# A Fourier layer and a token and channel mixer on one core: the 47-point products of the stream's last two units in three rounded passes, with the weight tasks on fewer steps and some early work in another order

## The chip, the core and the metric

The kernel runs on one core of a Trainium2 chip. Its engines work side by side, each through its own queue in order: TensorE (PE, with its weight loads as PEld), VectorE (DVE), ScalarE (ACT), GpSimd (POOL) and SyncE (SP), which issues most of the transfers (DMA). The metric is the device time of one execution in microseconds (us); the number that is compared is the median of several runs.

## The reference

For 8 batches of 3008 tokens with 256 channels, all in fp32:

```python
X = np.fft.rfft(x, axis=1)
Yr = Xr @ w_r - Xi @ w_i + b_r
Yi = Xr @ w_i + Xi @ w_r + b_i
Y  = soft_threshold(Yr, 0.01) + 1j * soft_threshold(Yi, 0.01)
x  = np.fft.irfft(Y, n=3008, axis=1)
h  = np.maximum(x.transpose(0, 2, 1) @ w_tok1, 0.0) @ w_tok2   # over tokens, 256 wide
u  = x + h.transpose(0, 2, 1)
out = u + np.maximum(u @ w_ch1, 0.0) @ w_ch2                   # over channels, 1536 wide
```

## The kernel before

The transform of length 3008 is done as 47 times 64. A *47-point product* multiplies a row of 120 sums or differences of inputs (13 rows a unit) by a constant matrix `f1`; its results go to DRAM (`a_d`) and come back, per pair of frequencies `kp` (12 pairs), for the 64-point step, the mix with `w_r` and `w_i`, the synthesis with the matrices `e` (the `inverse`, L501 and the passes in L208 to L210 with `pi` as output) and the first token product (`tokens`, output `gp`).

The batches are five units: 0 is one batch, done first in plain fp32 by `begin`; units 1, 2 and 3 are two batches each (512 columns) and unit 4 is one (256 columns), done by `stream`. In the stream most products are *rounded*: an operand is split into a high part (a cast on ACT) and a low part (a subtraction), and three matmuls high*high, high*low, low*high (`mm3`, L208 to L210) take the place of one fp32 matmul. The 47-point products are still plain fp32 (L278). The stream has 84 steps, one for each unit, `kp` and batch (24 each for units 1 to 3, 12 for unit 4). While a unit is in its steps, the 13 rows of the *next* unit's 47-point products are put between them by `row47`: it loads the input of row n+3 (`load`), forms sums and differences of row n+2 (`add`: the sums on POOL, L265; the differences on DVE, L266, or on POOL for units 3 and 4), and multiplies row n (`product`). Unit 1's own rows run late in `begin`.

Beside the steps the stream does *tasks*: it widens and splits the weights of the later stage (`w_ch1`, `w_ch2`, `w_tok2`, which come as pairs of 32-bit words: tile `wide`, DVE L175 to L182 and L720 to L731, split into `so`). Every task has a cost, and `pace`, the sum of costs over `TASK1 - TASK0` steps, says how much of them is due in a step from `TASK0` on. In unit 1's steps it also splits the synthesis matrices (`split_e`, tile `et`, ACT and DVE) and stores them (`es_d`) for the later units, and splits the token weights of unit 0 (`split_w`, ACT and POOL).

`begin` first does unit 0's 47-point products (L293), then, beside unit 0's steps, widens `w_tok1` and transforms it (L280, L281, stored as `a_w`), and from its step n = `NW` = 10 on reads `a_w` back (`load_w`, tile `aw`) and does its 64-point step (`transform`, L356). After the stream comes the *channel stage* (L905, L939 and the lines after them).

The written order isn't the order on the engines: a layer of the language sorts the instructions of each engine by readiness, except those pinned with `keep_in_program_order`; a tile pool with `bufs=n` makes the writer of a buffer wait for the readers of the buffer n before it. A queue never overtakes: what stands behind a waiting instruction waits with it.

## Time and profile before

| | |
|---|---|
| median of 3 runs | 2298.2 us (2296.5 to 2304.86) |
| the profiled execution: its time, its span | 2290.62 us, 2288.8 us |
| PE busy | 2252.3 us (98%), 11740 matmul records |
| DVE busy | 1951.2 us (85%) |
| ACT busy | 1630.9 us (71%) |
| POOL busy | 293.8 us (13%), all of it before 690 us |
| DMA | 407.87 MB, 178 GB/s in the mean |

All times of the trace count from the span's start; the profiled execution took 1.8 us more than its span. The span falls into `begin` (to 172 us), the stream (172 to about 680 us) and the channel stage (to the end). The stream's units begin, by their first L538 product, at 172.4, 311.8, 460.1 and 595.5 us.

### The profile page before, as it was taken

The numbers are of one execution on the slowest core, as the hardware profiler recorded it, in microseconds if no ns is written. First come the engines' busy times: TensorE is split into PE (matmuls) and PEld (weight loads), VectorE is DVE, ScalarE is ACT, GpSimd is POOL, SyncE is SP. The second block draws the span as 40 slices with busy tenths as digits, with TensorE's granted clock in tenths as the row PEclk, the third lists the DMA queues.
The fourth block names the chain that finished last, engine by engine and source line by source line (L and its number), as shares of the span: only waits on it lengthen the run. The fifth ranks groups of instructions, "written<-read, shape, count | busy, mean of one in ns | idle before, by whom it ended". The sixth has DMA issues, their size and how long they took to land.

```text
span 2288.8 us, 33922 instructions
## 1 busy us (share of the span) xinstructions
PE 2252.3 (98%) x11740; PEld 1911.8 (84%) x11740; DVE 1951.2 (85%) x3228; ACT 1630.9 (71%) x3103; POOL 293.8 (13%) x262
## 2 busy tenths in 40 slices
PE   8899999999999999999999999999999999999998
PEld 7767888899997888888888888888888888888887
DVE  7626877778747999989999998999998999998999
ACT  5446776666647777777777777777777777777776
POOL 0125755454330000000000000000000000000000
PEclk9999999999999999999999999999999999999999
DMA  7789978776677543454444445444454444444435
GB/s 215 226 281 304 303 240 274 240 243 219 192 225 243 162 153 121 147 171 152 139 144 146 124 148 177 147 141 149 120 160 142 153 146 142 139 147 143 143 109 159
DMA packets 205609, 407.87 MB, mean 178 GB/s; under 512 B 17093, under 2 KB 108829, under 8 KB 205437
## 3 DMA queue, kind: packets, MB, share of 16 engines
q1 hardware_dynamic: 175369, 351.69, 50.0%
q10 hardware_dynamic: 30068, 54.01, 7.0%
q8 instruction: 93, 1.52, 0.3%
q14 instruction: 79, 0.65, 0.1%
HBM read 303.00 MB, written 102.63 MB: 177 GB/s over the span
## 4 chain that ended last, share of the span: by engine, by line
PE 86%; DMA 5%; DVE 5%; ACT 2%; issue 1%; POOL 1%; SPq 1%; ACTq 0%; POOLq 0%; DVEq 0%
PE s L939 28%; PE sx L939 16%; PE sw L939 8%; PE pu L939 5%; PE pu L905 5%; PE fq L939 4%; PE p L554 4%; PE p L278 3%; PE px L538 2%; PE pm L554 2%; DMA x<-in_x 1%; PE gp L208 1%; PE gp L209 1%; PE gp L210 1%; DMA raw<-in_wt 1%
## 5 line engine op out<-in xcount | busy, mean ns | idle before, releaser
L939 PE MATMUL s<-rh,a2s 128*128 128x512 f32 (+1 forms) x2016 | 773.1, 386 | 1.5 <-ACT rh L154 0.8
L939 PE MATMUL sx<-ub,a 128*128 128x512 f32 (+1 forms) x1728 | 485.4, 389 | 1.8 <-DVE c L995 1.1
L939 PEld LDWEIGHTS s<-rh,a2s 128*128 128x128 f32 x2016 | 377.6, 188 | 78.8 <-ACT rh L154 1.6
L157 DVE TENSOR_TENSOR rl<-c,rh 128x512 fp32r<-128x512 f32 (+1 forms) x576 | 380.5, 674 | 38.6 <-ACT rh L154 30.8
L939 PE MATMUL s<-rl,a2s 128*128 128x512 f32 (+1 forms) x1008 | 389.2, 386 | 0.8 <-DVE rl L157 0.2
L154 ACT CAST rh<-c 128x512 fp32r<-128x512 f32 (+1 forms) x576 | 340.8, 613 | 57.0 <-DVE c L1036 18.3
L939 PEld LDWEIGHTS sx<-ub,a 128*128 128x128 f32 x1728 | 315.7, 188 | 62.6 <-DVE c L995 1.9
L939 PE MATMUL sw<-ub,a 128*128 128x512 f32 (+1 forms) x864 | 239.1, 385 | 0.4 <-ACT c L976 0.4
L939 PEld LDWEIGHTS s<-rl,a2s 128*128 128x128 f32 x1008 | 189.4, 188 | 40.0 <-DVE rl L157 2.9
L1064 DVE TENSOR_TENSOR uf<-s,uf 128x512 f32<-128x512 f32 (+1 forms) x288 | 194.0, 674 | 18.1 <-PE s L939 17.6
L154 ACT CAST rh<-r 128x512 fp32r<-128x512 f32 (+1 forms) x288 | 174.2, 612 | 37.5 <-PE s L939 25.6
L157 DVE TENSOR_TENSOR rl<-r,rh 128x512 fp32r<-128x512 f32 (+1 forms) x288 | 189.0, 672 | 4.1 <-ACT rh L154 3.1
L939 PEld LDWEIGHTS sw<-ub,a 128*128 128x128 f32 x864 | 160.8, 188 | 34.5 <-ACT c L976 0.8
L911 ACT COPY uf<-pu 128x470 f32<-128x470 f32 (+31 forms) x158 | 61.0, 415 | 121.3 <-PE pu L905 120.8
L905 PEld LDWEIGHTS pu<-g,b 96*128 96x128 f32 x1024 | 130.7, 191 | 4.1 <-DMA b<-b_d 0.7
L157 POOL TENSOR_TENSOR yl<-z,yh 128x512 fp32r<-128x512 f32 x84 | 114.1, 1359 | 129.7 <-ACT yh L154 128.0
L905 PE MATMUL pu<-g,b 96*128 96x94 f32 x1024 | 129.3, 271 | 0.3 <-DMA b<-b_d 0.3
L1039 DVE SCALAR_TENSOR_TENSOR rl<-c,rh 128x512 fp32r<-128x512 f32 (+1 forms) x144 | 97.4, 677 | 29.1 <-ACT rh L1038 27.9
L939 PE MATMUL fq<-ub,a 128*128 128x512 f32 (+1 forms) x432 | 121.6, 390 | 0.0
L939 PE MATMUL pu<-wt,gh 128*128 128x470 f32 (+1 forms) x424 | 116.7, 356 | 0.0
L976 ACT COPY c<-sw 128x512 f32<-128x512 f32 (+1 forms) x144 | 83.3, 579 | 42.5 <-PE sw L939 40.3
L970 ACT COPY fq<-sx 128x512 f32<-128x512 f32 (+1 forms) x144 | 81.1, 563 | 41.2 <-PE sx L939 39.4
(151 smaller groups left out, 4562.4 us busy)
## 6 DMA issues: line engine op xcount, KB each, us to landing
a2s<-a_d SPq DMA_DIRECT2D x336, 384.0 KB, 3.1
wt<-wt_d SPq DMA_DIRECT2D x32, 940.0 KB, 5.6
out<-uf SPq DMA_DIRECT2D x78, 256.0 KB, 3.1
x<-in_x SPq DMA_DIRECT2D x39, 480.0 KB, 6.2
a<-a_d SPq DMA_DIRECT2D x36, 512.0 KB, 5.8
b_d<-bt ACTq DMA_DIRECT2D x36, 512.0 KB, 4.2
wt<-wt_d SPq DMA_DIRECT2D x24, 752.0 KB, 5.2
a_d<-a ACTq DMA_DIRECT2D x36, 480.0 KB, 5.3
```

The lines of the kernel that those rows point to most:

```text
L154: S.copy(out=hi, in_=src)
L157: lo_eng.tensor_tensor(out=lo, in0=src, in1=hi.bitcast(F32), op=ALU.subtract)
L278: PE.matmul(pt[:120, o:o + w], lhsT=f1[:, i], rhs=sd[:, i], start=True, stop=True)
L538: PE.matmul(pt[:, o:o + 128], lhsT=a2[:, ab, b, t * 128:(t + 1) * 128], rhs=f2cols(2 * kp + ab), start=True, stop=True)
L554: PE.matmul(out, lhsT=xt[x][:, j, t], rhs=w_[:, wsel, t], start=start and t + i == 0, stop=t == 1 and i == 2, skip_group_check=True)
L905: m = PE.matmul(pt[:, s * TOKS:(s + 1) * TOKS], lhsT=b2[:, s, cs], rhs=g2[:, 0 if s0 + s == 0 else 1], start=False, stop=s == k - 1, skip_ ...
L911: S.copy(out=ufs[m][:, ct, lo - at:hi - at], in_=pt[:, lo - c0:hi - c0])
L939: m = PE.matmul(out, lhsT=w, rhs=x, start=start and n == 0, stop=n == 2, skip_group_check=True)
L970: S.copy(out=q, in_=x)
L976: S.copy(out=block(1, k), in_=w)
L1039: V.scalar_tensor_tensor(out=lo, in0=src, scalar=0.0, in1=hi.bitcast(F32), op0=ALU.max, op1=ALU.subtract)
L1064: V.tensor_tensor(out=o, in0=outs[r], in1=o, op=ALU.add)
```

## The change

It has these parts:

- `round`, a new call of `row47` one row ahead of the product, splits the sums and differences of units 3 and 4 (`FIRSTR = 3`) into `hi` (ACT) and `lo` (DVE), 2 x 512 columns a row for unit 3 and 2 x 256 for unit 4, and `stage1` multiplies them with the split constant `f1r` in three passes. `f1r` is split once, in `begin`.
- The tasks run over steps 16 to 78 in place of 3 to 82.
- The synthesis matrices are split in `begin`, after each `inverse` of unit 0, on ACT and POOL in place of ACT and DVE, and stored there; unit 1 reads them back as the later units do. `ef` has three buffers in the pool `early`, `et` three.
- In `begin`, `row47` stands ahead of `tokens` and `transform`, and at n = `NW` its transfers are issued after the loads of `a_w`.
- The first two turned tiles of unit 0 are copied in halves, by DVE and ACT.
- `f1` is loaded through ACT's queue; the pool `deep` lies below `wide` in memory; `ev` moves into `early`.

```diff
-FIRST47 = 7
-TASK0, TASK1 = 3, 82
+FIRST47, FIRSTR = 7, 3
+TASK0, TASK1 = 16, 78
...
+    f1r = mid.tile([120, 2, 2, 128], F32R, name="f1r")
...
-    DMA.dma_start(out=f1w, in_=io["f1"])
+    PUT.dma_start(out=f1w, in_=io["f1"])
...
+                if hi is not None:
+                    mm3(pt[:120, o:o + w], f1r[:, 0, i, :120], f1r[:, 1, i, :120], hi[:, i], sd[:, i], True, True)
+                elif pool is None:
...
-    def split_e(ef, kp):
-        et = wk.tile([128, 2, 2, 128], F32R, name="et")
-        split(et[:, 0], et[:, 1], ef, S, V)
+        et = wk.tile([128, 2, 2, 128], F32R, name="et", bufs=3)
+        split(et[:, 0], et[:, 1], ef, S, G)
...
             if kp < 2:
-                V.tensor_copy(out=a2.rearrange("p k b c -> p (k b c)"), in_=pt)
+                V.tensor_copy(out=flat[:, :C], in_=pt[:, :C])
+                S.copy(out=flat[:, C:], in_=pt[:, C:])
...
+        def round(g):
+            if g < NG and u >= FIRSTR:
+                sd, hi = sums_[g], wc["ys"].tile([120, 2, p.w], F32R, name="hi", bufs=2)
+                lo = wk.tile([120, 2, p.w], F32R, tag="o", name="lo", bufs=4)
+                split(hi, lo, sd, S, V)
+                sums_[g], his[g] = lo, hi
...
-        for k, call in ((n + 3, "load"), (n + 2, "add"), (n, "product")):
+        for k, call in ((n + 3, "load"), (n + 2, "add"), (n + 1, "round"), (n, "product")):
...
                     if u == 1:
                         wts_[kp] = split_w(raw_w.pop(kp), kp)
-                        ets[u, kp] = split_e(raw_e.pop(kp), kp)
                         load_we(kp + 2)
-                    else:
-                        ets[u, kp] = load_split_e(kp)
+                    ets[u, kp] = load_split_e(kp)
...
+                if n == NW + 4:
+                    split(f1r[:, 0], f1r[:, 1], f1w[:, :2], S, V)
...
-                    p.inverse(k, es.pop(k), ys[k], early)
-                    if k + 2 < KP:
-                        es[k + 2] = load_e(k + 2)
+                    while later:
+                        later.pop(0)()
+                    p.inverse(k, es[k], ys[k], early)
+                    split_e(es.pop(k), k)
+                    if k + 3 < KP:
+                        es[k + 3] = load_e(k + 3)
...
                 if n >= FIRST47 and done47["n"] < NG:
-                    row47()
+                    if n == NW:
+                        with tc.issue_after(wc["aw"].ins):
+                            row47()
+                    else:
+                        row47()
+                k = n - NW
+                if k >= 2:
+                    p.tokens(k - 2, wfs1.pop(k - 2), ys[k - 2])
+                if k >= 0:
+                    transform(k)
...
-    with tc.tile_pool(name="wide", bufs=1) as wide, tc.tile_pool(name="deep", bufs=1) as deep, tc.tile_pool(name="ys", bufs=6) as ysp:
+    with tc.tile_pool(name="deep", bufs=1) as deep, tc.tile_pool(name="wide", bufs=1) as wide, tc.tile_pool(name="ys", bufs=6) as ysp:
```

Three places show what this does to the engines' queues. Line numbers of the changed kernel are up to 18 higher for the same code. The first place is on PE in `begin`, at the first product of `transform` (`pw<-aw`). Before, and then with the change:

```order
L483 MATMUL pm<-wf_133,xf 128x256 x2
L483 MATMUL pm<-wsum,xf 128x256 x4
L501 MATMUL pi<-held,ef 128x256 x2
L483 MATMUL pm<-wf_133,xf 128x256 x2
L356 MATMUL pw<-aw,fw 64x256 x4
L278 MATMUL p_950<-sd,f_79 120x512
L278 MATMUL p_953<-sd,f_79 120x512
```

```order
L487 MATMUL pm<-wf_134,xf 128x256 x2
L487 MATMUL pm<-wsum,xf 128x256 x4
L505 MATMUL pi<-held,ef 128x256 x2
L281 MATMUL p_975<-sd,f_79 120x512
L281 MATMUL p_978<-sd,f_79 120x512
L359 MATMUL pw<-aw,fw 64x256 x4
L487 MATMUL pm<-wf_134,xf 128x256
```

Two 47-point products (`p<-sd`) moved from behind the first `pw` to ahead of it, and two products of the mix (`pm<-wf`) from ahead of it to behind it.

The second place is on DVE at the stream's entry, in steps 2 and 3 (`sd<-x` are differences of unit 2's inputs, `xs` and `xtl` belong to the 64-point step, `p` and `z` to the mix). Before, and then with the change:

```order
L545 TENSOR_TENSOR xs<-px,xs 128x256
L547 TENSOR_TENSOR xtl<-px,xth 128x512
L266 TENSOR_TENSOR sd<-x 120x512
L559 TENSOR_TENSOR p_1064<-pm,bias 128x512
L178 TENSOR_SCALAR wide<-raw 128x512
L266 TENSOR_TENSOR sd<-x 120x512
L545 TENSOR_TENSOR xs<-px,xs 128x256
```

```order
L549 TENSOR_TENSOR xs<-px,xs 128x256
L551 TENSOR_TENSOR xtl<-px,xth 128x512
L267 TENSOR_TENSOR sd<-x 120x512
L563 TENSOR_TENSOR p_1106<-pm,bias 128x512
L267 TENSOR_TENSOR sd<-x 120x512
L549 TENSOR_TENSOR xs<-px,xs 128x256
L551 TENSOR_TENSOR xtl<-px,xth 128x512
```

The task's instruction (`wide<-raw`) is gone from here; the two differences still stand ahead of the next step's `xs`.

The third place is on DVE in unit 2, from the `xs` of its fourth step on. Before, and then with the change:

```order
L545 TENSOR_TENSOR xs<-px,xs 128x256
L547 TENSOR_TENSOR xtl<-px,xth 128x512
L567 SCALAR_TENSOR_TENSOR z<-p_1063,z 128x512
L559 TENSOR_TENSOR p_1063<-pm,bias 128x512
L545 TENSOR_TENSOR xs<-px,xs 128x256
L547 TENSOR_TENSOR xtl<-px,xth 128x512
L567 SCALAR_TENSOR_TENSOR z<-p_1064,z 128x512
L559 TENSOR_TENSOR p_1064<-pm,bias 128x512
L178 TENSOR_SCALAR wide<-raw 128x470
L175 TENSOR_SCALAR wide<-wide 128x470
L179 SCALAR_TENSOR_TENSOR wide<-wide 128x470
L545 TENSOR_TENSOR xs<-px,xs 128x256
```

```order
L549 TENSOR_TENSOR xs<-px,xs 128x256
L563 TENSOR_TENSOR p_1106<-pm,bias 128x512
L551 TENSOR_TENSOR xtl<-px,xth 128x512
L157 TENSOR_TENSOR lo<-sd,hi 120x1024
L175 TENSOR_SCALAR wide<-wide 128x512
L571 SCALAR_TENSOR_TENSOR z<-p_1105,z 128x512
L179 SCALAR_TENSOR_TENSOR wide<-wide 128x512
L563 TENSOR_TENSOR p_1105<-pm,bias 128x512
L180 TENSOR_SCALAR wide<-wide 128x512
L157 TENSOR_TENSOR lo<-sd,hi 120x1024
L181 TENSOR_TENSOR wide<-raw,wide 128x512
L178 TENSOR_SCALAR wide<-raw 128x512
```

Twelve rows hold two steps before, and less than one step with the change: two subtractions `lo` of 1024 columns and a task lie between the step's own instructions.

## Rows read from the trace of the kernel before

**Rows 1.** The first line of the page, and the by-engine part of its chain of the work that ended last (shares of the span).

```profile
span 2288.8 us, 33922 instructions
...
PE 86%; DMA 5%; DVE 5%; ACT 2%; issue 1%; POOL 1%; SPq 1%; ACTq 0%; POOLq 0%; DVEq 0%
```

**Rows 2.** Busy time of each engine by stage. Columns: the stretch in us and its length; busy us of PE (instructions), PEld, DVE, ACT, POOL; the granted clock of TensorE as a share of full speed; DMA share; GB/s. The stretches are: all before the stream's first product; the entry to the stream; the rest of unit 1; unit 2; unit 3; and the channel stage.

```profile
0.00:172.40 172.40, 156.43 (x785) 120.69 (x786) 98.70 (x184) 85.72 (x154) 27.62 (x20) 0.97 0.81 241
172.40:205.00 32.60, 28.38 (x160) 22.67 (x158) 16.55 (x30) 18.08 (x39) 17.03 (x14) 0.90 0.97 310
205.00:311.80 106.80, 105.60 (x644) 88.81 (x645) 92.17 (x148) 78.44 (x169) 71.90 (x60) 1.00 0.88 293
311.80:460.10 148.30, 146.05 (x893) 123.21 (x893) 109.95 (x168) 99.77 (x203) 80.69 (x73) 1.00 0.78 249
460.10:595.50 135.40, 134.43 (x895) 123.22 (x894) 104.88 (x179) 92.96 (x193) 65.92 (x68) 1.00 0.69 222
...
690.00:2288.80 1598.80, 1590.75 (x7682) 1346.30 (x7682) 1475.01 (x2423) 1202.99 (x2241) 0.00 (x0) 1.00 0.48 148
```

**Rows 3.** What TensorE waited for between 20 and 172 us: us in total, times, the longest.

```profile
PE pw L356 <- DMA aw<-a_w: 3.8, 1, 3.8
PE px L468 <- ACT bt L504: 2.4, 1, 2.4
PE px L468 <- DVE a L458: 1.8, 1, 1.8
```

**Rows 4.** The timeline of the first 25 us: start us, us, engine, line, operation, names, size, count, and in brackets the idle time ahead of it and who ended it.

```profile
0.74 0.47 SPq L242 DMA_DIRECT2D f<-in_f  x1
...
22.27 1.28 DVE L458 COPY a<-pz 128x512 f32<-128x512 f32 x2
```

**Rows 5.** Groups of instructions by line and shape, over the whole span: count | busy us, mean ns of one | idle time ahead of them: the split of the synthesis matrices on DVE, and a POOL subtraction of the same 256 columns.

```profile
L548 POOL TENSOR_TENSOR xtl<-xs,xth 128x256 fp32r<-128x256 f32 x84 | 65.7, 782 | 78.2 <-ACT xth L546 76.0 <-DMA a<-a_d 1.8
...
L157 DVE TENSOR_TENSOR et<-ef,et 128x256 fp32r<-128x256 f32 x12 | 10.4, 863 | 4.1 <-ACT et L154 4.1
```

**Rows 6.** The same columns as in rows 2, in stretches of 20 us.

```profile
60.00:80.00 20.00, 19.12 (x97) 15.78 (x95) 19.22 (x33) 8.22 (x15) 4.51 (x3) 1.00 0.67 193
...
100.00:120.00 20.00, 16.18 (x73) 11.01 (x72) 7.21 (x10) 6.47 (x13) 4.31 (x3) 0.91 0.78 238
...
180.00:200.00 20.00, 16.84 (x90) 13.26 (x90) 8.08 (x14) 10.14 (x21) 10.71 (x9) 0.85 0.99 312
```

**Rows 7.** The timeline around the first product of the weights' transform (L356).

```profile
103.42 0.33 SPq L440 DMA_DIRECT2D x<-in_x  x1
103.91 3.32 SPq L348 DMA_DIRECT2D aw<-a_w  x3
...
105.66 1.03 PE L483 MATMUL pm<-wf,xf 128*128 128x256 f32 x4
...
110.51 1.09 PE L356 MATMUL pw<-aw,fw 128*64 128x256 f32 x8 [3.82 <-DMA aw<-a_w]
```

**Rows 8.** The timeline of the entry to the stream.

```profile
184.99 0.83 SPq L440 DMA_DIRECT2D x<-in_x  x2
...
185.91 0.43 DVE L178 TENSOR_SCALAR wide<-raw 128x512 uint32<-128x512 uint32 x1 [1.47 <-DMA raw<-in_moe_w_ch]
...
190.01 0.69 DVE L266 TENSOR_TENSOR sd<-x 120x512 f32<-120x512 f32 x1 [3.68 <-DMA x<-in_x]
...
190.15 1.69 POOL L265 TENSOR_TENSOR sd<-x 120x512 f32<-120x512 f32 x1 [5.19 <-DMA x<-in_x]
...
191.78 1.09 PE L278 MATMUL p<-sd,f 120*120 120x512 f32 x2 [1.85 <-DVE xtl L547]
```

**Rows 9.** Pieces of the chain that ended last, in order of time: start us, us, engine, line, count of records. One fp32 product (L278) is two records. At 341 us its operand has 512 columns a product and at 481 us 256; the rounded passes are L208 to L210, with 512 columns at 344 us and 256 at 640 us.

```profile
341.22 1.72 PE p L278 x4
...
344.54 0.24 PE gp L208
344.77 0.23 PE gp L209
345.01 0.23 PE gp L210
...
481.75 0.87 PE p L278 x4
...
640.61 0.12 PE pi L208
```

**Rows 10.** DVE and ACT time of the tasks (all instructions that touch the tile "wide"), in the columns of rows 2 (PE and PEld stand ahead of DVE and are zero; each engine's count is in brackets). The sum is over 172.4 to 690 us.

```profile
311.80:460.10 148.30, 0.00 (x0) 0.00 (x0) 56.20 (x69) 11.58 (x20) 1.00 0.78 249
460.10:595.50 135.40, 0.00 (x0) 0.00 (x0) 51.54 (x81) 11.88 (x24) 1.00 0.69 222
...
sum 517.60, PE 0.00 PEld 0.00 DVE 175.04 ACT 38.24; mean PE 0.00 PEld 0.00 DVE 35.01 ACT 7.65
```

**Rows 11.** DVE subtractions and sums by width: three groups of units 2 and 3 (columns as in rows 5), and the channel stage's subtraction, where POOL has no work (count: shortest/median/longest ns, first and last start).

```profile
L567 DVE SCALAR_TENSOR_TENSOR z<-p,z 128x512 f32<-128x512 f32 x48 | 33.0, 688 | 37.3 <-ACT z L566 37.0
...
L545 DVE TENSOR_TENSOR xs<-px,xs 128x256 f32<-128x256 f32 x48 | 20.1, 419 | 11.4 <-ACT xs L544 11.3
...
L157 DVE TENSOR_TENSOR so<-wide,so 128x470 fp32r<-128x470 f32 x8 | 7.5, 936 | 1.4 <-ACT so L154 1.1
...
L157 DVE TENSOR_TENSOR rl<-c,rh x576: 411/683/695, 702.1 to 2284.7; 128x512 fp32r<-128x512 f32 x185, 128x256 fp32r<-128x256 f32 x7
```

More of the change, by code (lines that the diff above doesn't have):

```diff
@@ L231, in ev @@
     def ev(shape, name):
-        return wk.tile(shape, F32, tag="ev", name=name, bufs=2)
+        return wc["early"].tile(shape, F32, tag="ev", name=name, bufs=2)
     def evs(shape, name):
@@ L263, in sum_diff @@
             return x
-        sd = wk.tile([120, 2, w], F32, tag="o", name="sd", bufs=4) if pool is None else wk.tile([120, 2, w], F32, tag=("xtl", "et")[g % 2], name="sd", bufs=(4, 2)[g % 2])
+        sd = wk.tile([120, 2, w], F32, tag="o", name="sd", bufs=4) if pool is None else wk.tile([120, 2, w], F32, tag=("xtl", "et")[g % 2], name="sd", bufs=(4, 3)[g % 2])
         eng.tensor_tensor(out=sd[:, 0], in0=x[:, 0], in1=x[:, 1], op=ALU.add)
@@ L267, in sum_diff, with stage1 @@
         return sd
-    def stage1(sd, dst, g, w, pool):
+    def stage1(sd, dst, g, w, pool, hi=None):
         n = GS if g < NG - 1 else N2 - GS * (NG - 1)
@@ L276, in stage1 @@
                 o = (i - i0) * w
-                if pool is None:
+                if hi is not None:
+                    mm3(pt[:120, o:o + w], f1r[:, 0, i, :120], f1r[:, 1, i, :120], hi[:, i], sd[:, i], True, True)
+                elif pool is None:
                     PE.matmul(pt[:120, o:o + w], lhsT=f1[:, i], rhs=sd[:, i], start=True, stop=True)
@@ L347, in load_w @@
             aw = wk.tile([128, 2, DT], F32, tag="lw", name="aw")
-        DMA.dma_start(out=aw, in_=src[:, 2 * kp:2 * kp + 2] if src is a_w else src[kp])
+        wc["aw"] = DMA.dma_start(out=aw, in_=src[:, 2 * kp:2 * kp + 2] if src is a_w else src[kp])
         return aw
@@ L363, in load_e @@
     def load_e(kp):
-        ef = wk.tile([128, 2, 128], F32, tag="le", name="ef")
+        ef = wc["early"].tile([128, 2, 128], F32, name="ef", bufs=3)
         DMA.dma_start(out=ef, in_=io["e"][kp].rearrange("p (i j) -> p i j", i=2))
@@ L376, in split_e @@
     def split_e(ef, kp):
-        et = wk.tile([128, 2, 2, 128], F32R, name="et")
-        split(et[:, 0], et[:, 1], ef, S, V)
+        et = wk.tile([128, 2, 2, 128], F32R, name="et", bufs=3)
+        split(et[:, 0], et[:, 1], ef, S, G)
         later.append(lambda: DMA.dma_start(out=es_d[kp], in_=et.rearrange("p a i j -> p (a i j)").bitcast(F32)))
-        return et
     def load_split_e(kp):
-        et = wk.tile([128, 2, 2, 128], F32R, name="et")
+        et = wk.tile([128, 2, 2, 128], F32R, name="et", bufs=3)
         DMA.dma_start(out=et.rearrange("p a i j -> p (a i j)").bitcast(F32), in_=es_d[kp])
@@ L456, in turn @@
             a2 = ld([128, 2, nb, C], "a2")
+            flat = a2.rearrange("p k b c -> p (k b c)")
             if kp < 2:
-                V.tensor_copy(out=a2.rearrange("p k b c -> p (k b c)"), in_=pt)
+                V.tensor_copy(out=flat[:, :C], in_=pt[:, :C])
+                S.copy(out=flat[:, C:], in_=pt[:, C:])
             else:
-                S.copy(out=a2.rearrange("p k b c -> p (k b c)"), in_=pt)
+                S.copy(out=flat, in_=pt)
             return a2
@@ L581, in beside @@
         p = parts_of(u)
-        xs, sums_ = {}, {}
+        xs, sums_, his = {}, {}, {}
         def load(g):
@@ L590, in add @@
                 sums_[g] = sum_diff(xs.pop(g), g, p.w, G, None, G if u > 2 else V)
+        def round(g):
[4 more added lines that the diff above has]
+                sums_[g], his[g] = lo, hi
         def product(g):
             if g < NG:
-                stage1(sums_.pop(g), p.a, g, p.w, None)
-        return SimpleNamespace(load=load, add=add, product=product)
+                stage1(sums_.pop(g), p.a, g, p.w, None, his.pop(g, None))
+        return SimpleNamespace(load=load, add=add, round=round, product=product)
     rows47 = [(u, g) for u in range(1, len(UNITS)) for g in range(NG)]
@@ L621, in stream @@
         a2s, xts, ys, ets = {}, {}, {}, {}
-        wts_, raw_w, raw_e = wc["wts"], {}, {}
+        wts_, raw_w = wc["wts"], {}
         def load_we(kp):
             if kp < KP:
-                raw_w[kp], raw_e[kp] = load_w(w_d, kp), load_e(kp)
+                raw_w[kp] = load_w(w_d, kp)
         def need(i):
@@ L798, in begin @@
             w1 = prepare_w1(early, after)
-            es, xts = {k: load_e(k) for k in range(2)}, {}
+            es, xts = {k: load_e(k) for k in range(3)}, {}
             DMA.dma_start(out=sc, in_=io["scale"])
```

5 lines of the change are left out of this document (removed).

## The prediction, made before the changed kernel was run

> **What bounds the kernel now.** I read the chain that ended last first: 86% of it is TensorE's own work [rows 1]. Then the stages: in the channel stage PE is busy for 1590.75 of 1598.8 us [rows 2], and no instruction of that stage changes, so whatever the change brings lies in the first 690 us. There unit 2 leaves PE idle for 148.3 - 146.05 = 2.3 us and unit 3 for 1.0 us: both are bound by PE's matmuls. The two other places that are left are the waits in `begin` [rows 3] and the entry to the stream, where PE works 28.38 of 32.6 us at a mean granted clock of 0.90 [rows 2]. The reader is to see one more thing in those rows: DVE is busy for 109.95 us of unit 2 and 104.88 us of unit 3, 74% and 77%. It is off the path, but it has only some 35 us to spare in each, and the change spends them.
>
> **The products.** One fp32 product of 512 columns takes 1.72 / 2 = 0.86 us on the chain, one of 256 columns 0.87 / 2 = 0.43 us; three rounded passes take 0.24 + 0.23 + 0.23 = 0.70 us and 3 x 0.12 = 0.36 us [rows 9]. Unit 3 has 13 rows x 2 products of 512 columns, unit 4 the same number of 256: 26 x 0.16 + 26 x 0.07 = 4.2 + 1.8 = **6.0 us less** of PE work, 4.2 of it in unit 2's stretch (the rows go beside the unit ahead of theirs) and 1.8 in unit 3's. That is worth its full size only while PE stays the bound there.
>
> **What DVE pays for it.** First `lo`. A DVE operation takes 419 ns for 256 columns and 688 ns for 512 [rows 11], 269 ns for 256 more; so 1024 columns are some 688 + 2 x 269 = 1.23 us. An operation that reads SBUF alone takes longer while POOL works: `so`, of 470 columns, has a mean of 936 ns, whereas the same subtraction of 512 columns in the channel stage, where POOL has no work, has a median of 683 ns and never takes more than 695 [rows 11]. I add 0.3 us for that to each `lo`: 13 x 1.53 = 19.9 us in unit 2's stretch, 13 x 0.99 = 12.9 us in unit 3's. Second, the tasks: 175.04 us of DVE [rows 10] over 79 steps are 2.22 us a step, over 62 steps 2.82; 24 steps hold 67.8 us in place of 56.2 (unit 2) and 51.54 (unit 3). DVE's need becomes 109.95 + 11.6 + 19.9 = 141.4 us in unit 2 and 104.88 + 16.3 + 12.9 = 134.1 us in unit 3, **275.5 us** together. PE's own time there would be 283.7 - 6.0 = 277.7 us. DVE would have to be busy for 99% of it, in order, beside a PE that waits for it in every step (`xs`, `xtl`, `p`, `z`). Two stretches bound what it can do: in the rest of unit 1 DVE is busy for 92.17 of 106.8 us, 86%, and PE loses only 1.2 us; in the channel stage it is busy for 92% and PE loses 8 of 1599 us [rows 2]. So nothing shows a cost up to 92%, and nothing here runs at 99%. The lower bound of the cost is nothing (shorter waits for POOL would do), the upper one is DVE held at 92%: 275.5 / 0.92 = 299.5 us, 21.8 over PE's time. I take 97%, nearer to the lower end since `lo` is made a whole row ahead of its product: 275.5 / 0.97 = 284.0 us, **6.3 us** over PE's time. The saving of the products is then eaten whole, and the two units last as long as before. ACT pays too, 13 casts of 1024 columns and 13 of 512, but it has 48 us to spare in unit 2 and 42 in unit 3 [rows 2] against some 16 if a cast takes what a DVE operation of its width does: nothing.
>
> On POOL and DVE the Trainium skill (GPSIMD Engine Reference, Key points) says that GpSimd shares its SBUF interfaces with VectorE and that they contend when the DVE instruction has two SBUF inputs; `lo` and the second halves of the tasks are such instructions. The trace agrees (936 ns against 683). By that rule moving work to a DVE beside a busy POOL is dearer than its columns, which speaks against the change; it is the third rival below.
>
> **The entry to the stream.** DVE stands in order at 185.91 us behind a task's load (1.47 us) and at 190.01 behind an input of unit 2 (3.68 us); the 64-point step's `xs` and `xtl` are queued behind it, and PE then waits 1.85 us at 191.78 [rows 8]. From 180 to 200 us the granted clock is 0.85 [rows 6], so part of it ran at 1.2 GHz in place of 2.4 just after that wait. Idle time here is 32.6 - 28.38 = 4.2 us, the clock takes (1 - 0.90) x 32.6 = 3.3 us: 7.5 us in all [rows 2]. The change takes the tasks, their loads and their stores out of steps 3 to 15 and the split of the matrices (863 ns each) [rows 5] out of unit 1. The inputs, whose transfers share DMA engines that are 97% busy here [rows 2], should land earlier. The order of the differences ahead of `xs` stays, so not all of it goes. Bounds: nothing and 7.5 us; I take **5 us less**, nearer the upper end because both things that DVE waits for are transfers and traffic falls.
>
> **The wait for `a_w`.** PE ends its work at 106.69 us and waits 3.82 us for the first `aw`, whose loads were issued at 103.91, just behind an input [rows 7]. With the change that input goes behind them, and two 47-point products (2 x 0.86 us) stand ahead of `pw`, while four records of the mix (1.03 us) [rows 7] move behind it: the wait shrinks by 0.7 us through the order and by what the input took from the loads. The granted clock of 100 to 120 us is 0.91 [rows 6], 1.8 us lost, which may go too. Bounds 0 and 3.8 + 1.8 = 5.6 us; I take **3 us less**.
>
> **The split in `begin`.** Twelve ACT casts and twelve POOL subtractions (782 ns each) [rows 5] come into a stretch where DVE is busy for 19.22 of 20 us at 60 to 80 us [rows 6] and where PE once waits 2.4 us for an ACT that follows DVE [rows 3]. POOL itself has room (27.62 of 172 us) [rows 2]. SP now also issues twelve stores there, each of which waits for POOL, ahead of loads of `w_tok1` and inputs; the buffers of `ef` and `et` are three, so a store is seldom the first to be late. If each POOL subtraction holds DVE for half its length, that is 12 x 0.39 = 4.7 us, of which only the part before 100 us, where DVE is full, can reach PE. Bounds 0 and 4.7; I take **1 us more**.
>
> **The start.** SP issues `f1` for 0.47 us ahead of the inputs [rows 4], and unit 0's products run at the pace of these issues; on ACT's queue that time goes. The two copies that PE waits for take 1.28 us on DVE [rows 4]; half of each goes to an idle ACT. Together **0.8 us less** (0 to 1.1).
>
> **At nothing:** the split of `f1r` (one ACT and one DVE instruction under the inputs' pace); the reading back of `es_d` in unit 1, which takes the place of a load and a store there; the pools' order, since `deep` then lies where `begin` frees memory first and the tasks' tiles come later. If that cover is gone, a late first split of the token weights would hold ACT and POOL at the entry, inside that term's lower bound.
>
> **The sum:** -6.0 + 6.3 - 5 - 3 + 1 - 0.8 = -7.5 us. The profiled execution's 2290.62 us becomes 2283; it lies 7.6 us under the median of the runs, 2298.2, from which I forecast 2298.2 - 7.5, about **2290 us** (0.3% less). A difference of 0.5%, 11.5 us, is about what a measurement tells from none: 2286.7 and 2309.7 us are the marks.
>
> **Rivals.**
> *A, DVE keeps up.* If the subtractions rarely meet POOL, the 0.3 us each fall away (26 x 0.3 = 7.8 us), DVE needs 268 us, 96% of PE's time, and units 2 and 3 keep the whole 6.0 us. Then -6.0 - 5 - 3 + 1 - 0.8 = -13.8: **2284 us**, down to 2276 with the upper bounds of the other terms. For it: PE lost almost nothing at 92%. Against it: no stretch is that full.
> *B, the entry stays.* The three buffers that unit 2's inputs use are also those in which unit 0's last results lie, and an input is issued only when a sum has freed its buffer: the issue at 184.99 comes between two waits of POOL for inputs [rows 8]. If that, not traffic, sets the pace, the 5 us don't come: **2295 us**.
> *C, DVE becomes the bound.* At 92% DVE the two units take 299.5 us, 15.8 more than before; with the other terms (-7.8) the kernel is at **2306 us**, slower than before. The turning point is a DVE share of 275.5 / (283.7 + 7.8) = 94.5%; slower by 0.5% needs 275.5 / 303 = 91%. For it: twelve rows of DVE's queue hold two steps before and less than one after, and all of it is in order. Against: tasks can slip into units 1 and 4.
>
> **Chances.** The forecast (2286 to 2294) 0.38, A 0.32, B 0.13, C 0.17. Faster by over 0.5%: A whole and a fourth of the forecast's, 0.40; slower by over 0.5%: two thirds of C, 0.12; within 0.5%: 0.48. The range runs from 2270 (A with all upper bounds, and a little) to 2307 (C at 92%): some 0.07 lie below and 0.13 above.
>
> **What would show it.** L208 to L210 with `p` as output at 0.70 and 0.36 us a product; units 2 and 3 lasting about 284 us together, with DVE busy near 97% and `lo` near 1.5 us; PE's wait at the first `pw` under 2 us; the entry to the stream shorter by about 5 us with a granted clock near 1; no new PE wait over 2 us in `begin`. Units 2 and 3 at 278 us would show A, over 292 us C. I am wrong in kind if DVE's tasks don't crowd at all, or if a late transfer in `begin` costs more than all these terms.

## The result, and the profile after

The changed kernel takes **2310.4 us** in the median (2307.5 to 2315.3) against 2298.7 us of the kernel before in the same series: the ratio is **1.0055**, with a 95% interval of 1.0044 to 1.0067. By the ratio it is slower by 0.55%, 12.6 us. The forecast was 2290 us with a range from 2270 to 2307: wrong in sign and outside the range. One of the eight runs of the kernel before took 2837.0 us; the ratio goes by the other seven.

The first line of the page after and its chain by engine answer to [rows 1]:

```profile
span 2310.1 us, 34084 instructions
...
PE 85%; DVE 6%; DMA 4%; ACT 2%; issue 2%; SPq 1%; POOL 0%; ACTq 0%; POOLq 0%; DVEq 0%
```

The stages of the changed kernel, in the columns of [rows 2]: all before the stream, its entry (32.6 us), the rest of unit 1, unit 2, unit 3, and the channel stage.

```profile
0.00:180.30 180.30, 158.22 (x774) 119.47 (x775) 100.92 (x183) 88.71 (x167) 38.65 (x32) 0.95 0.84 244
180.30:212.90 32.60, 27.66 (x148) 22.01 (x147) 15.26 (x26) 17.57 (x39) 19.26 (x16) 0.88 0.89 281
212.90:325.40 112.50, 110.31 (x668) 94.07 (x667) 63.61 (x105) 73.31 (x148) 67.76 (x59) 0.97 0.77 245
325.40:480.80 155.40, 147.40 (x920) 131.53 (x919) 141.19 (x205) 111.60 (x223) 90.99 (x72) 0.97 0.77 251
480.80:618.80 138.00, 134.06 (x920) 123.22 (x919) 122.14 (x208) 101.33 (x212) 69.11 (x69) 1.00 0.74 235
710.00:2310.10 1600.10, 1592.30 (x7698) 1348.27 (x7696) 1475.80 (x2424) 1204.46 (x2244) 0.00 (x0) 1.00 0.48 149
```

Against [rows 2] `begin` is 7.9 us longer, unit 1 (its entry and its rest) 5.7, unit 2 7.1 and unit 3 2.6. To see which of these differences count, both kernels were traced a second time. `begin` and units 1, 2 and 3 of the second execution of the changed kernel, and behind them those of the kernel before:

```profile
0.00:176.40 176.40, 158.06 (x775) 119.99 (x775) 101.86 (x183) 89.17 (x167) 36.46 (x32) 0.95 0.83 249
176.40:321.90 145.50, 137.34 (x814) 115.34 (x814) 77.43 (x131) 90.91 (x186) 87.03 (x74) 0.96 0.80 253
321.90:477.50 155.60, 147.60 (x920) 131.68 (x919) 141.19 (x205) 111.67 (x223) 91.09 (x72) 0.97 0.76 250
477.50:615.60 138.10, 134.38 (x921) 123.31 (x920) 122.07 (x208) 101.18 (x212) 68.88 (x69) 1.00 0.74 235
```

```profile
0.00:174.40 174.40, 157.24 (x785) 121.22 (x785) 98.90 (x184) 85.80 (x154) 27.59 (x20) 0.97 0.83 239
174.40:316.60 142.20, 135.16 (x802) 112.02 (x803) 108.90 (x177) 96.52 (x207) 89.28 (x74) 0.96 0.89 289
316.60:465.20 148.60, 146.14 (x894) 123.31 (x894) 109.93 (x168) 99.95 (x203) 81.10 (x73) 1.00 0.77 249
465.20:600.20 135.00, 134.43 (x895) 123.20 (x894) 103.89 (x179) 92.87 (x193) 65.42 (x68) 1.00 0.71 224
```

Units 2 and 3 repeat within 0.4 us, so the 7.1 and 2.6 us by which they are longer (7.0 and 3.1 in the second traces) are real. `begin` and unit 1 vary by up to 4 us from one execution to the next; there only the medians of the timed runs settle a few microseconds. The traced executions of the kernel before took 2290.6 and 2292.9 us, 5 to 8 under its median.

What TensorE waits for in `begin` of the changed kernel answers to [rows 3]:

```profile
PE p L281 <- ACT a L285: 3.8, 1, 3.8
PE p L283 <- DVE wide L182: 3.6, 3, 2.2
PE pm L487 <- ACT a L285: 3.1, 1, 3.1
PE px L472 <- ACT bt L508: 3.0, 1, 3.0
```

The wait for `a_w` is gone, the one for `bt` was there before, and the others, 10.5 us together, are new or grown. The first and the last lie close together between 80 and 100 us, where PE works 13.23 of 20 us and the granted clock is 0.74 in the mean (first row):

```profile
80.00:100.00 20.00, 13.23 (x49) 9.71 (x48) 11.80 (x18) 6.18 (x12) 5.39 (x5) 0.74 0.64 196
340.00:360.00 20.00, 16.43 (x106) 14.61 (x105) 19.13 (x22) 11.82 (x23) 13.56 (x11) 0.97 0.62 194
360.00:380.00 20.00, 19.42 (x109) 17.18 (x109) 15.78 (x26) 13.84 (x28) 9.41 (x8) 0.86 0.82 278
420.00:440.00 20.00, 17.04 (x93) 14.67 (x92) 19.46 (x28) 13.28 (x28) 11.13 (x9) 0.91 0.67 212
460.00:480.00 20.00, 19.38 (x130) 17.50 (x129) 19.05 (x31) 15.05 (x33) 10.35 (x11) 1.00 0.80 258
```

The other lines are of unit 2. DVE is nearly full in three of them (19.13, 19.46 and 19.05 of 20 us); PE stops for long in the first two of these, and loses 0.6 us in the third. DVE's queue at the first of these stops, and PE's wait there:

```profile
351.85 0.92 DVE L180 TENSOR_SCALAR wide<-wide 128x512 uint32<-128x512 uint32 x1
352.69 2.31 DVE L157 TENSOR_TENSOR lo<-sd,hi 120x1024 fp32r<-120x1024 f32 x1
354.93 0.68 DVE L181 TENSOR_TENSOR wide<-raw,wide 128x512 f32<-128x512 f32 x1
355.53 1.50 DVE L178 TENSOR_SCALAR wide<-raw 128x512 uint32<-128x512 uint32 x1
356.95 1.75 DVE L182 TENSOR_TENSOR wide<-wide 128x512 f32<-128x512 f32 x1
358.62 0.41 DVE L549 TENSOR_TENSOR xs<-px,xs 128x256 f32<-128x256 f32 x1
```

```profile
359.77 1.62 PE L542 MATMUL px<-f,a 128*128 128x128 f32 x6 [3.57 <-DVE xtl L551]
```

One `lo` of 2.31 us and four instructions of the tasks stand ahead of `xs`; `xtl` is behind them, and PE waits 3.57 us. The second place is the same with a `lo` of 2.29 us, and PE waits 2.96 us for `p`. These rows are not only many, they are also slow: the five ahead of `xs` take 7.16 us, and the shortest instructions of the same lines and widths in this trace 0.41, 1.21, 0.68, 0.41 and 0.67 us, 3.4 in all. The difference of 3.8 us is about what PE waits here. POOL works for all but 1.7 of the 6.8 us from the first of these starts to that of `xs`.

### The profile page after: what moved, and what is told of

The parts are those of the page before. It is cut to its first block, busy times and chain, and to the rows that moved or that the text cites. A ratio compares the mean times of both kernels' runs of the same rounds, so it can differ in the third digit from the quotient of the medians.

```text
span 2310.1 us, 34084 instructions
## 1 busy us (share of the span) xinstructions
PE 2258.7 (98%) x11792; PEld 1923.6 (83%) x11792; DVE 1970.1 (85%) x3243; ACT 1648.5 (71%) x3132; POOL 317.1 (14%) x274
## 4 chain that ended last, share of the span: by engine, by line
PE 85%; DVE 6%; DMA 4%; ACT 2%; issue 2%; SPq 1%; POOL 0%; ACTq 0%; POOLq 0%; DVEq 0%
PE s L957 28%; PE sx L957 16%; PE sw L957 8%; PE pu L957 5%; PE pu L923 5%; PE fq L957 4%; PE p L558 3%; PE px L542 2%; PE pm L558 2%; PE p L281 2%; PE gp L209 1%; PE gp L208 1%; PE gp L210 1%; DMA raw<-in_wt 1%; PE pm L487 1%
```

## The experiments

Every kernel here but before_again holds the small parts (the order in `begin`, the copies in halves, `f1` on ACT's queue, the pools) unless the table says otherwise. Each ratio is to the kernel before, timed beside it (its median was 2296.6 to 2298.7 us). The intervals are about ±0.0011, for some ±0.0017, so a difference between two variants of less than about 3.5 us (4.5 with the wider intervals) says nothing. Differences are given as the difference of the ratios times 2298 us.

| kernel | tasks on steps | 47-point products | split of the matrices | else | ratio [95%] |
|---|---|---|---|---|---|
| the change | 16-78 | rounded | begin, POOL | | 1.0055 [1.0044, 1.0067] |
| no_round | 16-78 | fp32 | begin, POOL | | 1.0043 [1.0029, 1.0056] |
| tasks_wide | 3-82 | rounded | begin, POOL | | 1.0007 [0.9996, 1.0018] |
| e_late | 16-78 | rounded | unit 1, DVE | | 1.0035 [1.0022, 1.0047] |
| narrow_late | 16-78 | fp32 | unit 1, DVE | | 1.0030 [1.0018, 1.0041] |
| order_alone | 3-82 | fp32 | unit 1, DVE | | 0.9987 [0.9979, 0.9996] |
| old_order | 3-82 | fp32 | unit 1, DVE | old order in begin | 1.0006 [0.9996, 1.0016] |
| three_pass | 3-82 | rounded | unit 1, DVE | | 0.9982 [0.9973, 0.9992] |
| change_dve | 16-78 | rounded | begin, DVE | | 1.0018 [1.0009, 1.0027] |
| split_dve | 3-82 | rounded | begin, DVE | | 0.9956 [0.9939, 0.9972] |
| pool_store | 3-82 | rounded | begin, POOL | stores by POOL | 1.0005 [0.9992, 1.0018] |
| dve_pool_store | 3-82 | rounded | begin, DVE | stores by POOL | 0.9972 [0.9963, 0.9981] |
| act_store | 3-82 | rounded | begin, POOL | stores by ACT | 0.9978 [0.9969, 0.9988] |
| n_hl4 | 3-82 | fp32 | unit 1, DVE | four `hl` | 0.9981 [0.9973, 0.9989] |
| narrow_hl4 | 16-78 | fp32 | unit 1, DVE | four `hl` | 1.0005 [0.9995, 1.0016] |
| hi1_hl4 | 3-82 | rounded | unit 1, DVE | four `hl`, one `hi` | 0.9958 [0.9941, 0.9974] |
| all_best | 3-82 | rounded | begin, DVE | four `hl`, one `hi` | 0.9957 [0.9943, 0.9971] |

**The parts, one by one.** Theory 1: the tasks and `lo` crowd DVE in units 2 and 3. Theory 2: the split in `begin` holds the inputs back.

```diff
-FIRST47, FIRSTR = 7, 3
-TASK0, TASK1 = 16, 78
+FIRST47, FIRSTR = 7, 9          # no_round, narrow_late, order_alone
+TASK0, TASK1 = 3, 82            # tasks_wide, order_alone, three_pass
```

The comments name the first runs that have an edit; the table says it for all. In e_late and all that split in unit 1, `split_e` and its loads are those of the kernel before.

no_round. 

> The changed kernel with its 47-point products of units 3 and 4 left in fp32 (no hi, no lo); tasks over steps 16 to 78, the matrices split in begin, and all the rest stay. Theory T1, the crowd on DVE (the subtractions lo at 2.3 us beside tasks that are denser): units 2 and 3, 293.5 us together with the change, come down to 284 to 287 us although PE's own work grows by 6 us, and the kernel lies 6 to 9 us under the changed one, near 2302. Theory T2, the split in begin (its stores and POOL work hold the inputs back): begin stays at 180 us and unit 1 at 145 us. Rival, that the rounding itself is worth its 6 us and the loss comes from the tasks' window alone: units 2 and 3 get longer, 296 us or more.

tasks_wide. 

> The changed kernel with the tasks back over steps 3 to 82. T1: DVE in units 2 and 3 needs some 120 us and 110 us in place of 141 and 122, and the two units fall from 293.5 to 279 to 284 us, now with the rounding worth its 6 us; unit 1 (145 us) gets no shorter or 2 to 6 us longer, since the tasks come back to its entry; the kernel lies 5 to 12 us under the changed one. T2: begin stays at 180 us. Rival, that lo alone costs what the units lost: they stay over 290 us.

e_late. 

> The changed kernel with the synthesis matrices split in unit 1's steps, on ACT and DVE, as before. T2: begin falls from 180.3 to 170 to 174 us, the waits of 3.8 and 3.0 us at 83 and 89 us and that of 3.1 us at 127 us are gone and so is the stretch at half clock behind them; the kernel lies 5 to 9 us under the changed one. T1: units 2 and 3 stay at 290 to 296 us. Rival, that begin grew for another reason (row47 ahead of transform, copies in halves): begin stays at 178 us or more.

order_alone. 

> The kernel before with the small parts of the change alone: row47 ahead of tokens and transform with the loads of a_w issued first, the copies in halves, f1 on ACT's queue, the order of the pools; no rounding, tasks over 3 to 82, matrices split in unit 1. If T1 and T2 are all that the change costs, nothing is left here that is slower: 2290 to 2298 us, begin at 168 to 172 us, PE's wait at the first pw under 2 us. Rival, that the order in begin itself costs: begin over 175 us and the kernel over 2302.

three_pass. 

> The small parts (row47 ahead, copies in halves, f1 on ACT's queue, pools) and the rounded products, with the tasks on steps 3 to 82 and the synthesis matrices split in unit 1 as before: the earlier order_alone (2293.7 us) plus the rounding. Theory 1 (rounding pays where the tasks leave DVE room; with tasks on 3 to 82 units 2 and 3 lasted 281.6 us with it and 285.2 without): units 2 and 3 near 281.6 us, 2290 us, about 0.3% under the kernel before. Rival (lo costs DVE what PE saves under any spread of the tasks; adding up the single steps of the first four runs gives this): units 2 and 3 at 285 us, 2294 us.

narrow_late. 

> The small parts and the tasks on steps 16 to 78; no rounded products, matrices split in unit 1 as before. Theory 1a (denser tasks alone hold the step's instructions up, at a DVE share of only 80%): units 2 and 3 near 293 us as in no_round, some 8 us over order_alone, about 2302 us. Rival 1b (density costs only together with lo): units 2 and 3 near 285 us, about 2294 us.

The path from the kernel before to the change, one part at a time: the small parts -3.0 us (order_alone), the tasks on 16 to 78 **+9.9** (narrow_late), the rounding +1.1 (e_late), the split in `begin` **+4.6** (the change). With tasks on 3 to 82 the rounding is worth -1.1 us (three_pass against order_alone). Undone in the change itself, the task window gives back 11.0 us (tasks_wide). Theory 1a holds: the window costs about 10 us without any `lo` too. no_round missed its 2302 us by 6 for that reason. three_pass hit the rival's 2294 us, but not by its stages: unit 2 (144.9 us) is as short as Theory 1 said and unit 3 (138.4) is not. Units 2 and 3 of tasks_wide:

```profile
328.10:473.40 145.30, 142.74 (x921) 127.49 (x920) 125.72 (x179) 106.95 (x212) 89.50 (x71) 1.00 0.78 250
473.40:609.60 136.20, 133.01 (x920) 122.86 (x919) 115.19 (x191) 97.73 (x207) 68.12 (x69) 1.00 0.70 223
```

Unit 2 lasts 144.6 to 145.8 us in all eight traces with rounding and tasks on 3 to 82, against 148.1 to 150.1 in the five without rounding: the 4 us of the products are there, though the timed runs show only the 1.1. In the change (155.4 us) PE is idle for 8.0 us in place of 2.6, and its own work takes 147.40 us in place of 142.74 at a clock of 0.97. So of 10.1 us between the two, 5.4 are waits and 4.7 slower matmuls, in stretches where PE had just stopped (0.86 at 360 to 380 us, 0.91 at 420 to 440 us). Without `lo` unit 2 is no longer (149.7 us in narrow_late, 149.2 in order_alone), and the crowding shows in unit 3: 142.7 us against 136.0, 4.3 of the 6.7 us as PE's idle time. The other 3 us of the 9.9 lie ahead of unit 2, where one trace says little. In unit 3 the products wait for ACT (`bt` behind an instruction of a task), and ACT's casts for DVE. The first row is PE's wait in unit 3 of narrow_late, the next two are ACT's waits for DVE; in order_alone the three are 0.2, 7.8 and 7.6 us:

```profile
PE p L281 <- ACT bt L509: 3.1, 3, 1.3
```

```profile
ACT so L154 <- DVE wide L182: 12.3, 7, 2.8
ACT xth L551 <- DVE xs L550: 8.9, 11, 1.4
```

**Where the split in begin costs.**

```diff
-        split(et[:, 0], et[:, 1], ef, S, G)
+        split(et[:, 0], et[:, 1], ef, S, V)                        # split_dve, change_dve, dve_pool_store
-        later.append(lambda: DMA.dma_start(out=es_d[kp], ...
+        later.append(lambda: G.dma_start(out=es_d[kp], ...         # pool_store, dve_pool_store
+        later.append(lambda: PUT.dma_start(out=es_d[kp], ...       # act_store
```

pool_store. 

> tasks_wide (the change with tasks on steps 3 to 82, 2298.9 us) with the twelve stores of the split matrices issued by POOL itself in place of SP; split work and its engines as in the change. Theory 2 (a loop through SP: the store waits on SP for POOL's et, POOL's et stands behind POOL's sum of an input, and the next inputs stand behind the store): the stalls at 75 to 92 us go down to the one of about 2.5 us that the kernel before has, the stream begins at 171 to 174 us in place of 184, and the time falls by about 5 us to 2294. Rival 2b (the work of the split itself, POOL beside a full DVE and casts on ACT): the stream still begins after 178 us, 2298 us.

split_dve. 

> tasks_wide (2298.9 us) with the subtractions of the split matrices in begin on DVE in place of POOL; stores on SP as in the change. Theory 2c (POOL is what the early split costs: its subtractions stand behind sums that wait for inputs, and stretch DVE's own): the stream begins at 171 to 174 us, the time falls to three_pass's 2294. Rival 2d (the early split costs through its casts on ACT, its transfers and DVE's own fullness up to 80 us, whoever subtracts): the stream begins after 175 us, 2299 us or, as DVE gets 12 x 0.42 = 5 us more to do where it is full, up to 2303.

change_dve. 

> The change with one thing undone: the subtractions of the matrices' split in begin stand on DVE, not on POOL; tasks on 16 to 78, rounding and all else as in the change (2310.4 us, 1.0055). Theory 2c (POOL's place costs 12 us, as between tasks_wide and split_dve): 2298 us, the stream begins at 167 to 172 us. Rival (the two costs overlap, since the late start of the stream only shifts what the dense tasks hold up): 2304 us.

dve_pool_store. 

> split_dve (2286.9 us, 0.9956) with the twelve stores of the split matrices issued by POOL in place of SP: the control of pool_store (2299.0, 1.0005). If issuing them costs POOL nothing that matters, 2287 us, and pool_store says that the split on POOL costs its 12 us without any store on SP. If the issuing itself costs, 2292 to 2299 us, and pool_store says nothing on SP.

act_store. 

> tasks_wide (2298.9 us, 1.0007) with the twelve stores on ACT's queue in place of SP's; the split stays on POOL. Theory 2 (stores that wait on SP for POOL hold the inputs back): 2288 to 2294 us, unless ACT's own instructions now stand behind the same waits. Theory 2e (POOL's queue itself, in which the split stands among the sums of the inputs): 2299 us or more.

On DVE the early split is worth 6.0 us (split_dve against three_pass), which neither theory had expected; on POOL it costs 5.7 us (tasks_wide against three_pass). The place on POOL alone is 11.7 us there and 8.5 us in the change (change_dve), so the two costs mostly add. A part of it is a knot of three queues, which SP's and POOL's rows of the changed kernel show:

```profile
66.96 0.38 SPq L442 DMA_DIRECT2D x<-in_x  x1
...
76.37 0.35 SPq L382 DMA_DIRECT2D es_d<-et  x1
76.83 1.62 SPq L442 DMA_DIRECT2D x<-in_x  x2
```

```profile
73.22 2.44 POOL L266 TENSOR_TENSOR sd<-x 120x512 f32<-120x512 f32 x1 [6.73 <-DMA x<-in_x]
75.62 0.73 POOL L157 TENSOR_TENSOR et<-ef,et 128x256 fp32r<-128x256 f32 x1
83.44 1.68 POOL L266 TENSOR_TENSOR sd<-x 120x512 f32<-120x512 f32 x1 [7.09 <-DMA x<-in_x]
```

POOL's sum waits until 73.22 for an input issued at 66.96. The split of a matrix stands behind that sum; the store on SP waits for the split, until 76.37; the next two inputs stand behind the store, are issued at 76.83, and the next sum waits 7.09 us for them. Only one or two inputs go round the loop at a time. SP's waits for these stores before 172 us, in the change and with the split on DVE (change_dve):

```profile
SPq L382 <- POOL et L157: 33.6, 10, 7.7
```

```profile
SPq L382 <- DVE et L157: 11.7, 7, 5.5
```

These waits are no price: SP waits as long for other things where there is no early split (33.0 us for DVE's differences in order_alone). The price comes from the runs. act_store takes the stores off SP and leaves the split on POOL: 6.7 us less than tasks_wide, its `begin` 172.5 us in place of 184.0 (tasks_wide's traced execution lies 7 us over its median). The other 5.1 us up to split_dve stay with POOL. pool_store broke the same loop (its `begin` 174.5 us) and gained nothing in time (Theory 2's 2294 us missed). Its control, dve_pool_store, lies between the two cases that were expected: issuing the twelve stores may cost POOL 3.7 us, which the intervals don't tell from none. With all stores on POOL the split on POOL still costs 7.6 us against DVE (pool_store against dve_pool_store), so the stores on SP are some 4 to 7 of the 11.7 us. On transfers that GpSimd issues the Trainium skill (SBUF — State Buffer, its note on the "DVE blocks DMA" trap) says that their descriptors are written by GpSimd, which a DVE operation in a 2-port mode can lock out; no row here shows whether that happened. What the last 5 to 8 us are, POOL's place behind the sums or its subtractions beside DVE, is left open.

**The order in begin, and the entry to the stream.**

```diff
-        return wk.tile(shape, F32R, tag="hl", name=name, bufs=3)
+        return wk.tile(shape, F32R, tag="hl", name=name, bufs=4)   # all with four hl; x and wide likewise
-                sd, hi = sums_[g], wc["ys"].tile([120, 2, p.w], F32R, name="hi", bufs=2)
+                sd, hi = sums_[g], wc["ys"].tile([120, 2, p.w], F32R, name="hi", bufs=1)   # hi1_hl4, all_best
```

In old_order, `tokens`, `transform` and `row47` stand as in the kernel before.

old_order. 

> order_alone (2293.7 us) with the order of tokens, transform and row47 in begin put back to that of the kernel before; left of the change are the copies in halves, f1 on ACT's queue and the pools. Theory 4 (the wait for a_w taken away is given back: order_alone has no wait at the first pw, but a new one of 1.8 us at 118 us and a unit 1 of 142.9 us where the kernel before has 139.4): the wait of about 3.8 us at the first pw is back, unit 1 is near 140 us, the time within 1 us of order_alone's 2294. Rival 4b (the prediction's term holds): the time is 3 us over it, 2297 us.

n_hl4. 

> order_alone (2293.7 us) with four buffers in place of three for the tiles hl, in which inputs of the next units, unit 0's last results and some tasks lie. Theory 3 (the prediction's rival B: the inputs at the entry to the stream are issued only when a sum has freed one of three buffers): DVE's waits for inputs at the entry shrink, PE's busy time in the first 32.6 us of the stream rises from 26.6 to 29 us or more, the time falls by 2 to 4 us. Rival 3b (the transfers are slow because the DMA engines are 94% busy there): entry and time as in order_alone.

narrow_hl4. 

> narrow_late (tasks on steps 16 to 78, 2303.4 us) with four buffers hl in place of three. In n_hl4, where the tasks' loads are at the entry to the stream, a fourth buffer brought two inputs 5 us earlier and the time 1.4 us. Theory 3c (without the tasks' loads there the buffers set the pace of the inputs: in the trace of the change the DMA engines were down to 36 GB/s at 194 us while DVE waited for an input): DVE's waits for inputs at the entry fall from 13 us to 9 or less and PE's idle time in the first 32.6 us from 6.6 to 4, the time falls by 2 to 4 us, to 2300. Rival 3d (the inputs land late for another reason): no change, 2303.

hi1_hl4. 

> three_pass (2294.1 us, ratio 0.9982) with four buffers hl and one buffer for hi in place of two, to make the room. If the gains of three_pass and n_hl4 (0.9981) over order_alone (0.9987) add up: ratio 0.9975, 2292 us. If the single buffer of hi holds the cast of the next row up until the product of this one is done, units 2 and 3 get longer: 2296 us.

all_best. 

> The change with tasks on 3 to 82, the split on DVE, four buffers hl and one hi: split_dve (2286.9 us, 0.9956) plus what hi1_hl4 has over three_pass (2286.7 against 2294.1 us). If the gains add up: 2280 us, ratio 0.992. If both take away the same waits for inputs in begin: 2286 us.

The order is worth 4.4 us (order_alone against old_order), so Theory 4 falls by the time; the wait that the order removes is back in old_order:

```profile
PE pw L359 <- DMA aw<-a_w: 4.7, 1, 4.7
```

Something is given back all the same. At the entry to the stream ACT now stands behind the load of unit 0's token weights (`aw<-w_d`), a 47-point product's copy stands behind ACT's cast of them, and PE waits for that copy. Rows of ACT and PE in the changed kernel:

```profile
196.48 0.62 ACT L154 CAST wt<-aw 128x512 fp32r<-128x512 f32 x1 [5.02 <-DMA aw<-w_d]
198.33 0.59 ACT L285 COPY a<-p 120x512 f32<-120x512 f32 x1
198.98 2.08 PE L542 MATMUL px<-f,a 128*128 128x128 f32 x8 [2.68 <-ACT a L285]
```

ACT's wait for this load at the entry is 2.5 to 6.8 us in all seventeen traces with the new order, and there is none in the three with the old one (before, before_again, old_order). PE works 26.63 of the first 32.6 us of the stream in order_alone and 28.99 in old_order.

The fourth buffer is worth 5.7 us where the tasks are narrow (narrow_hl4 against narrow_late) and 1.4 us, within the intervals, in n_hl4. With the rounding, hi1_hl4 is 5.5 us under three_pass, more than was expected, and beats the kernel before by 0.42% (0.9958); a single `hi` costs nothing that can be seen. But the place is not the one that Theory 3c named: DVE's waits for inputs at the entry are 11.2 us in narrow_hl4 and 13.0 in narrow_late, not 9, while `begin` ends at 165.2 us in place of 173.6 and unit 3 lasts 138.6 us in place of 142.7 (the traced executions lie 4 us under and 4 us over their medians, so the sizes are rough). all_best is no better than either half of it, which fits that early split and fourth buffer take away the same waits; its one trace doesn't show which.

The last two here are the second traces, shown above.

before_again. 

> The kernel before, a second trace. If stages repeat: begin 172.4, unit 1 139.4, unit 2 148.4, unit 3 135.4 us within 1 us each. If the first trace was a lucky execution (it lay 8 us under the median): begin or unit 1 longer by 3 to 8 us.

after_again. 

> The changed kernel, a second trace. If stages repeat: begin 180.3, unit 1 145.1, unit 2 155.5, unit 3 138.0 us within 1 us each; else the spread tells which stage differences count.

## Why the prediction was wrong, step by step

**The products: right.** Three passes take 3 x 233 ns = 0.70 us at 512 columns and 3 x 118 ns = 0.35 us at 256 (medians of 63 and 65 passes, from one start to the next), as taken. Unit 2 is 4 us shorter where nothing else is in the way, as worked out. Of the 1.8 us in unit 3 nothing can be seen: 134.1 to 138.9 us with rounding, 134.4 to 136.0 without.

**What DVE pays: the step that failed.** Its need in unit 2 came out as forecast, 141.4 us and 141.19 measured, in part by luck: `lo` took 21.1 us there and 19.9 were taken, but these were eleven of 1024 columns and two of 512 in place of thirteen of 1024. In unit 3 the need was 122.14 us, 12 less than the 134.1 forecast, so DVE had more room than was thought. What failed was the conversion into time, "275.5 / 0.97 = 284.0 us" with the lower mark "nothing shows a cost up to 92%". Units 2 and 3 last 293.4 us, past the 292 us that the prediction named for rival C, at a DVE share of (141.19 + 122.14) / 293.4 = 90%, and narrow_late costs the 9.9 us at 81%. A share over a unit is a mean, and DVE has its queue in bursts: two stretches of 20 us, at 96 and 97%, hold both long waits of unit 2; a third, at 95%, costs nearly nothing. The mark of 92% came from the channel stage, which has none of these steps and no tasks. What decides in these rows is how many microseconds of other work stand ahead of the step's own `xs`, `xtl` and `p`, and that had been shown in the rows of the order: "twelve rows of DVE's queue hold two steps before and less than one after" was written under rival C and priced at 17 in 100. The row of all `lo` of the changed kernel (shortest, median and longest in ns, first and last start):

```profile
L157 DVE TENSOR_TENSOR lo<-sd,hi x26: 672/1216/2353, 288.6 to 586.6; 120x1024 fp32r<-120x1024 f32 x13, 120x512 fp32r<-120x512 f32 x13
```

The longest took 2.35 us against the 1.23 us worked out for one alone. The Trainium skill (GPSIMD Engine Reference, Key points) names contention of GpSimd with VectorE's instructions that have two SBUF inputs. The trace agrees: the five `lo` of over 2 us all run beside POOL for 1.2 us or more, though some of 1.21 and 1.22 us do nearly as long. The 0.3 us taken for it was too little, 1.69 us in the mean of the thirteen `lo` of 1024 columns against 1.53, and it missed the extremes: the two of 2.31 and 2.29 us stand ahead of the long waits. How much of these waits is POOL's doing and how much the number of rows stays open, as no run takes POOL's sums away; `lo` of 2.31 us occur in tasks_wide too, where unit 2 has 2.6 us of idle PE in all.

**The entry: failed too, in part as rival B had it.** Five us were to go with the tasks. In the first 32.6 us of the stream PE works 27.66 us at a clock of 0.88, before 28.38 at 0.90 [rows 2]: nothing gained. The DMA share did fall, from 0.97 to 0.89. One input is issued at 186.67 and lands some 7.1 us later, with a DMA share of 0.92 to 1.02 from 188 to 194 us: for that one traffic counts (the next takes 4.7 us). The next three are issued only at 195.69, after DVE's difference and POOL's sum have freed a buffer (SP waits 4.5 us there for the one and 1.1 for the other), while the DMA share from 194 to 196 us is 0.25: traffic does not hold these. The rows of SP and of DVE there, in the changed kernel:

```profile
186.67 0.39 SPq L442 DMA_DIRECT2D x<-in_x  x1
195.69 1.25 SPq L442 DMA_DIRECT2D x<-in_x  x3
```

```profile
193.85 0.69 DVE L267 TENSOR_TENSOR sd<-x 120x512 f32<-120x512 f32 x1 [4.48 <-DMA x<-in_x]
200.41 0.69 DVE L267 TENSOR_TENSOR sd<-x 120x512 f32<-120x512 f32 x1 [5.26 <-DMA x<-in_x]
```

The second of these waits is rival B's mechanism. But a fourth buffer alone did not shorten this stretch either, so what paces it beyond the buffers stays open. PE's own longest wait there, 2.68 us, is neither of the two: it hangs on the late token weights shown above. The prediction had that at nothing, unless the pools' order gave no cover (then "a late first split of the token weights would hold ACT and POOL at the entry"). With nothing won at the entry, the window of the tasks is all cost: the same work in 62 steps. And the new order in `begin`, not the window, brought the wait for the token weights.

**The wait for `a_w`: right; the start: not seen.** 3.8 us less were forecast for the order, `f1` and the copies together; order_alone measures 3.0, and the order alone 4.4. The 0.8 us of the start don't show: old_order, which has `f1` and the copies, is at 1.0006.

**The split in `begin`: mis-sized, by the bound's own reason.** One us was taken, 0 to 4.7 the bounds; it is 4.6. The bounds were made from what the subtractions take from DVE. The stores were named, with the remark that one "is seldom the first to be late"; SP waits 33.6 us for POOL in ten of them, ahead of the inputs, and moving them to ACT's queue gave 6.7 us back (act_store against tasks_wide). The prediction's own warning, "if a late transfer in `begin` costs more than all these terms", is close to what the traces show at 76 to 89 us.

**The sum.** Tasks, products and entry were to be -6.0 + 6.3 - 5 = -4.7 us and are +9.9 + 1.1 = +11.0; the split +1 and is +4.6; the rest -3.8 and is -3.0. The three misses, 15.7 + 3.6 + 0.8 = 20.1 us, are the way from -7.5 to +12.6. (A slip beside it: with all upper bounds rival A comes to 2298.2 - 20.2 = 2278 us, not 2276.)

## What to carry to other kernels

Read an engine's room from the stretches in which its queue stands ahead of the bound engine's next operand, not from its share of a stage: here a DVE share of 81 to 90% over two units cost 10 us because the same tasks came on fewer steps. When work is moved to another engine, follow what waits for its result on every queue: a store that waits on the loading queue passes the wait on to all loads behind it, and a split that is worth 6 us on one engine cost 6 on another. And spread side work over as many steps as there are, since taking it away from one crowded place gains only if what waits there was waiting for it. When a wait is gone, look for it further on: the new order in `begin` saved 4.4 us although a new wait came up at the entry.

## What the runs showed that was not expected

The same instruction at the same width, `lo` of 1024 columns, took from 1.21 us (at 378.30) to 2.35 us (at 346.40) in one execution. Units 2 and 3 repeat within 0.4 us between executions, while `begin` and unit 1, which lean on transfers, vary by up to 4 us with the same program. And behind the stops of PE of 3 to 4 us the granted clock of the stretch was lower (0.74 at 80 to 100 us, 0.86 at 360 to 380 us, 0.91 at 420 to 440 us, means between the levels of 2.4 and 1.2 GHz): in unit 2 that was nearly half of what was lost.
